# A second quarter of the input loaded by GpSimd instead of SyncE, two more quarters and one weight block asked for at other steps

## Chip, cores and metric

The kernel runs on 1 core of one Trainium2 chip. The metric is the device time of one execution in microseconds (us), the median over runs. A core has five instruction streams here: TensorE (PE, with its weight loads listed as PEld), VectorE (DVE), ScalarE (ACT), GpSimd (POOL) and SyncE (SP). SP does nothing but ask for transfers (DMAs); POOL asks for some too, on a queue of its own. Both queues are served by the same 16 DMA engines of the core.

## The reference

One layer of a mixer with adaptive layer norm: L = 2048 tokens, D = 448 channels, N = 256 states, F = 1792 hidden units, all float32.

```python
mod = (silu(c) @ w_mod).reshape(1, 6, 1, 448)        # w_mod is 448 x (6*448)
sa, ca, ga, sb, cb, gb = (mod[:, k] for k in range(6))
h = layernorm(x) * (1 + ca) + sa
x = x + ga * A_ref(h, ...)      # S4D: K[d,l] = 2 Re sum_n C exp(A dt l); long convolution by FFT; + h*D_skip
h = layernorm(x) * (1 + cb) + sb
x = x + gb * B_ref(h, ...)      # token mixing: w2.T gelu(w1.T layernorm(h) + b1) + b2
```

`A_u` is the input x (2048 x 448, 3.7 MB). `w_mod` is used in six blocks of 448 x 448, one for each of the six modulations.

## The kernel before, in words

The first half of the kernel builds the convolution kernel of the S4D layer from its 448 x 256 parameters (the "steps"), and transforms the input beside it (the "rows" and "columns"). The second half is the token MLP, a stream of large matmuls. The change lies in the first 70 us.

**Steps.** The steps are numbered s = 0 to 55 (NHALF = 56), half a group of 16 channels each. A step s consists of:

- `st_phase(s)` on PE: matmuls into two PSUM tiles, `xe` and `xg` (line 621; two buffers of each). It is issued one step ahead, so step s holds `st_phase(s + 1)`.
- `st_step(s)`: six activations on ACT (lines 677 to 682, the sines and cosines), two products on POOL (`G`, lines 684 and 685), and four on DVE (`E`, lines 686, 687, 689 and 690).
- `between()`, called between the second and the third of the DVE products: other DVE work is put in there. For 2 <= s < 8 that is `u_stats(2s)` and `u_stats(2s + 1)`, the layer norm's statistics of two of the 16 input rows in `xt` (lines 513 and 514).
- `st_kgen(s - 2)` on PE: 64 small matmuls from `E` and `G` (line 711).

Every eighth step begins with a set, `window(s)`: the exponentials of eight steps in a row (`st_exponents` on PE, `st_exp` on ACT, line 644; `st_mag2` on POOL, lines 660 and 665). The one before step 0 is called the first set here, the one before step 8 the second. In the first set, `u_stats(0)` to `u_stats(3)` are done at e = 4 to 7.

**Input.** `xt` is a tile of 128 partitions x 16 rows x 450. `x_load(r0, n, eng)` loads rows r0 to r0 + n with four DMAs, one for each group of 32 partitions, on the queue of `eng`. Four rows are called a quarter: four DMAs of 224 KB. Before the change the first quarter is asked for by POOL within `first_chain`, the second in two halves by SP after it (8 DMAs of 112 KB), the third by POOL behind step 1, the fourth by POOL behind step 2.

**Weights of the modulations.** `wm_load(k, tile)` asks for one block of `w_mod` (784 KB) on SP's queue. `modulation(k, half)` (lines 498 and 502 on PE) uses it: block 1 in steps 4 and 5, block 2 in steps 6 and 7, block 0 in the second set. `late` is a table by step: what stands at s is asked for by SP when the program comes to step s.

**Order.** The order of each engine's instructions is the order of the program (`manual_schedule`), so a wait holds up everything behind it on that engine. SP's order is written out by hand as well, up to step 8: it runs ahead of the others until a transfer has to wait for its tile, for its data or for earlier transfers. In the first set it moves the parameters of the first groups: `lex` and `lph` straight from SBUF (line 867), the rest through DRAM (`pars`, stored on line 871, read by `load` on lines 607 and 611). At s = 4 it asks for eight `lex` loads for the second set.

Of the kernel before, what the change touches and what calls it, by code (L numbers as in the profile page):

```python
# [220 lines left out]
def tile_adaln_s4d_mixer(ctx, tc, i, out):  # L221
# [20 lines left out]
    with ExitStack() as es:  # L242
        V, S, G, T = nc.vector, nc.scalar, nc.gpsimd, nc.tensor
# [53 lines left out]
        def x_load(r0, n, eng=nc.sync):  # L297
            for g in range(4):
                to = xt[32 * g : 32 * g + 32, r0 : r0 + n, 0:D]
                eng.dma_start(to, x.rearrange("(n g r) d -> g n r d", g=4, r=16)[g, :, r0 : r0 + n])  # L300
# [22 lines left out]
        def wm_load(k, tile):  # L323
            wms[k] = tile
            nc.sync.dma_start(wms[k], i["w_mod"][:, k * D : (k + 1) * D].rearrange("(q p) d -> p q d", p=PP))
# [11 lines left out]
        def wm_slot(k):  # L337
            w = wm0.rearrange("p k d -> p (k d)")[0:PP]
            return w[:, 4 * D * (k % 4) : 4 * D * (k % 4 + 1)].rearrange("p (q d) -> p q d", q=4)
# [1 line left out]


        late = {
            4: lambda: wm_load(2, wm_slot(2)),
            7: lambda: wm_load(0, wm_slot(0)),
            6: lambda: [
                nc.sync.dma_start(wu, i["WU"]),
# [114 lines left out]
        def logs(root=False):  # L462

            for a, s, u, xa, ya in tmp.values():
                S.activation(u, ya, AF.Square)
                S.activation(s, s, AF.Ln)
                S.activation(u, u, AF.Ln, bias=1.0)
            if root:
                S.activation(rs, mv[:, :, 1], AF.Ln, bias=eps_t)
                S.activation(rs, rs, AF.Exp, scale=-0.5)  # L470
            for q, (a, s, u, xa, ya) in tmp.items():
                S.activation(a, a, AF.Exp, bias=ldt[:, q : q + 1])
            tmp.clear()

        def angle():

            for a, s, u, xa, ya in tmp.values():
                S.activation(xa, ya, AF.Arctan)
# [134 lines left out]
        def load(g, exps):  # L613
            load_up(g, exps)
            load_lo(g, exps)
# [323 lines left out]
        par_load(1, par_names[2:4])  # L939
        for g in (1, 2):  # L940
            load(g, False)
        x_load(4, 2)
        x_load(6, 2)
        wm_load(1, wm_slot(1))
        remainder()

# [13 lines left out]
        def more(n):  # L960

            for _ in range(n):
                if next(rest, None) in ("logs", "end"):
                    return
# [26 lines left out]
        def window(s):  # L991
            if s:
                aside.append(True)
            angle()
            logs(s == 8)
            if s == 8:
                u_scale()
                u_table(0)
                u_table(1)

            if s == 0:
                st_exponents(s)
            for e in range(BATCH):
                st_exp(s + e)

                if e + 1 < BATCH:
                    st_exponents(s + e + 1)
                else:
                    st_phase(s)
                mellow()  # L1010
                flush(dve)
                flush(act)
                if s == 8 and e == 0:
                    tt(mod[1], mod[1], mod[2], ALU.mult)
                if s < 32:
                    more(WPACE[s // 8][e])
                if s == 0 and e >= 4:
                    u_stats(e - 4)
                if s == 8 and e in (3, 4):
                    modulation(0, e - 3)  # L1020
                if s == 8 and e == 5:

                    G.tensor_tensor(mod[0], mod[0], mod[2], ALU.mult)
                if s and e < (2 if s <= 32 else 1):
                    st_kgen(s - (2 if s <= 32 else 1) + e)
                elif e == 5:
                    if s == 8:
                        yks[0] = y0.tile([P, 32, DC], F32, tag="yk", name="yk0")
                    st_s1(s > 16)

                for k, e0 in ((4, 1), (5, 3), (3, 6)) if s == 16 else ():
                    if e in (e0, e0 + 1):
                        modulation(k, e - e0)

                if s == 8:
                    warm(7)
                if s in (8, 16):
                    some(u_rows, rows, (2, 2, 2, 2, 2, 0, 1, 1)[e])
                elif s == 24 and e != 5:
                    some(u_cols, cols, 1)  # L1040

                if s >= 40 and e == 2:
                    piece(False, True)
                if s >= 40 and e == 4:
                    piece(pieces[0] < NP, True)
                if s == 0 and e > 1:
                    st_mag2(e - 2)
                elif s and (e < 2 or s >= 32):
                    st_mag2(s + e)
                if s == 0 and e == 3:  # L1050
                    for r in range(4):
                        dsk_copy(r)
            aside.clear()
            if s == 0:

                S.activation(one, one, AF.Sin)
# [6 lines left out]
        for s in range(tail):  # L1063
            if s == 32:
                early.close()
                fp = es.enter_context(tc.tile_pool(name="fp", bufs=2))
                m2p.append(right("m2l", BATCH - 3))
                yks[1] = fp.tile([P, 32, DC], F32, name="yk1", bufs=1)
                for n in range(3):
                    pc_load(n)  # L1070
            if s % 2 == 0 and 0 < s and s // 2 + 2 < NG:
                load(s // 2 + 2, False)
            if s == 8:
                first.close()
            if s in late:
                late[s]()
            if s < NHALF and s % BATCH == 0:
                window(s)
                if s == 0:
                    gp_ = right("gp", 3)  # L1080
            if s % BATCH == 4:
                for g in range(s // 2 + 2, min(s // 2 + 6, NG)):
                    load(g, True)

            def between():
                flush(dve)
                if 2 <= s < BATCH:
                    for r in range(2 * s, 2 * s + 2):
                        u_stats(r)
                if s < len(pace):  # L1090
                    more(pace[s])

            mellow()
            if s >= NHALF:
                flush(dve)
                mellow()
            else:
                if s < 32 and s % BATCH > 1:
                    st_kgen(s - 2)
                if s % BATCH < 2:  # L1100
                    warm(10)
                if (s + 1) % BATCH:
                    st_phase(s + 1)
                elif s + 1 < NHALF:
                    st_exponents(s + 1)
                if s == 7:
                    warm(10)

                if s > 32 and s % BATCH:
                    st_kgen(s - 1)  # L1110
                st_step(s, between)
            flush(act)
            if s == NHALF:
                st_kgen(s - 1)


            if s in (1, 2):
                x_load(4 + 4 * s, 4, G)
            free = s > 7 and not st_s1(s % BATCH == BATCH - 1)
            if s + 2 < 32 and (s + 2) % BATCH > 1 and s + 2 > 5:  # L1120
                st_mag2(s + 2)

            if 3 < s < 8:
                modulation(s // 2 - 1, s % 2)
            if s == 7:
                par_load(2)

            if 8 <= s < 16 and free:
                some(u_rows, rows, 2 if s % 2 else 3)
            if s == 12:  # L1130
                par_load(3)
            if s == 16:
                spec.close()
                up = early.enter_context(tc.tile_pool(name="up", bufs=2))
                for n in range(4):
                    u_load(n)
            if 17 <= s < 32 and free:
                some(u_cols, cols, 2 if s < 24 else 3)
            if s == 31:
                flush(dve)  # L1140
                flush(act)
            if s > 32:
                piece(pieces[0] < NP and (s % 2 == 1 or s >= NHALF))
            if s == 34:

                for t in (ft, b1, b2):
                    V.memset(t, 0.0)
                nc.sync.dma_start(ft, i["FT"])
                nc.sync.dma_start(b1, i["B_b1"].rearrange("(t p) -> p t", p=P))
                nc.sync.dma_start(b2, i["B_b2"].rearrange("(t p) -> p t", p=P))  # L1150
# [52 lines left out]
    with ExitStack() as es:  # L1203
        es.enter_context(tc.manual_schedule(engines={ENG.PE, ENG.Activation, ENG.DVE, ENG.Pool}))
        V, S, G = nc.vector, nc.scalar, nc.gpsimd
# [192 lines left out]
```

## Time and profile before

| what | value |
|---|---|
| median of 3 runs | 697.69 us (696.94 to 703.69) |
| profiled execution | 699.5 us |
| its span, first to last instruction | 697.7 us |
| its mean granted TensorE clock | 0.988 |
| busy in the span | PE 646.5 us (93%), ACT 448.5 (64%), DVE 424.1 (61%), POOL 274.7 (39%) |
| DMA | 128.04 MB, mean 184 GB/s |

The profiled execution is one of its own; 1.8 us of its time lie outside the span. In the lists below every line gives the start and the duration in us, the engine, the line of the kernel, the operation and its operands; in square brackets stands how long the engine had been idle before it, and what ended that. "SPq" is a DMA instruction on SP's own queue.

### The profile page before, as it was taken

Reading aid. Unit: us, or ns where it says so; the run is one execution under the profiler, and the core shown is the slowest. Engines: PE = TensorE matmul, PEld = TensorE weight load, DVE = VectorE, ACT = ScalarE, POOL = GpSimd, SP = SyncE. Lnnn points to the kernel's source line nnn. Section 1 sums busy time; section 2 is a strip of 40 time slices with the busy share of each in tenths; the row PEclk is TensorE's granted clock in tenths of the full one; section 3 lists DMA queues with packets and bytes.
Section 4 is the critical chain, followed back from the end, with each engine's and each line's share of the span. In section 5 each row is a group of like instructions: output and inputs, shape, how many; then the busy total and the mean of one; then the engine's idle time right before and its main releaser. Section 6 shows DMA issues by size and latency. Waiting matters only on the chain.

```text
span 697.7 us, 18532 instructions
## 1 busy us (share of the span) xinstructions
PE 646.5 (93%) x7314; PEld 486.1 (70%) x7314; DVE 424.1 (61%) x811; ACT 448.5 (64%) x841; POOL 274.7 (39%) x364
## 2 busy tenths in 40 slices
PE   0868999999988899999999989999999999999997
PEld 0444454455545676676789747778999999999996
DVE  7877889787575584857744368777622354444431
ACT  5787698899879899999766568877422332222220
POOL 6694669588588767777546200000000000000000
PEclk9998999999999999999999999999999999999999
DMA  7595647588785486554579899974683445555640
GB/s 183 178 194 143 214 163 241 212 234 268 213 266 165 126 170 170 145 157 120 142 235 301 257 278 244 236 177 135 174 247 108 146 132 159 159 158 165 169 129 28
DMA packets 101894, 128.04 MB, mean 184 GB/s; under 512 B 13547, under 2 KB 85231, under 8 KB 101807
## 3 DMA queue, kind: packets, MB, share of 16 engines
q1 hardware_dynamic: 100606, 123.31, 63.0%
q0 software_dynamic: 1200, 3.54, 2.4%
q8 instruction: 58, 0.95, 0.6%
q14 instruction: 30, 0.24, 0.1%
HBM read 91.46 MB, written 34.87 MB: 181 GB/s over the span
## 4 chain that ended last, share of the span: by engine, by line
PE 68%; ACT 10%; DMA 8%; DVE 6%; issue 4%; POOL 3%; SPq 1%; DVEq 0%; ACTq 0%; POOLq 0%
PE xe L621 7%; PE acc L1222 7%; PE o L1365 6%; PE o L1364 6%; PE o L1366 6%; PE acc L1223 6%; PE acc L1224 6%; PE kg L711 6%; DMA si<-in_SK_dram 3%; PE xg L621 3%; PE pu L542 2%; PE pu L574 2%; PE vv L820 2%; PE kx L804 2%; PE vv L821 2%
## 5 line engine op out<-in xcount | busy, mean ns | idle before, releaser
L206 ACT CAST whi<-w 128x896 fp32r<-128x896 f32 x64 | 59.8, 938 | 134.9 <-PE o L1365 84.6
L215 DVE TENSOR_TENSOR wlo<-w,whi 128x896 fp32r<-128x896 f32 x64 | 68.1, 1088 | 43.1 <-ACT whi L206 36.8
L684 POOL TENSOR_TENSOR G<-mag,gs 128x512 f32<-128x512 f32 x56 | 71.9, 1283 | 50.9 <-ACT gs L680 47.1
L1222 PE MATMUL acc<-h3h,whi 128*128 128x448 f32 x224 | 82.7, 369 | 0.8 <-ACT h3h L1273 0.8
L1223 PE MATMUL acc<-h3l,whi 128*128 128x448 f32 x224 | 81.5, 364 | 0.7 <-DVE h3l L1280 0.5
L1365 PE MATMUL o<-ul,whi 128*128 128x448 f32 x224 | 81.3, 363 | 0.0
L1364 PE MATMUL o<-uh,whi 128*128 128x448 f32 x224 | 81.2, 362 | 0.0
L1224 PE MATMUL acc<-h3h,wlo 128*128 128x448 f32 x224 | 80.7, 360 | 0.0
L1366 PE MATMUL o<-uh,wlo 128*128 128x448 f32 x224 | 80.6, 360 | 0.0
L711 PEld LDWEIGHTS kg<-E,G 128*32 128x32 f32 x3584 | 56.6, 114 | 32.3 <-issue 22.2
L711 PE MATMUL kg<-E,G 128*32 128x64 f32 x3584 | 66.4, 228 | 6.7 <-issue 6.1
L685 POOL TENSOR_TENSOR G<-mag,gs 128x512 f32<-128x512 f32 x56 | 71.8, 1282 | 0.0
L621 PE MATMUL xg<-tab,lph 64*128 64x512 f32 x112 | 62.3, 556 | 5.1 <-ACT gs L680 2.4
L621 PE MATMUL xe<-tab,lph 64*128 64x512 f32 x112 | 62.2, 555 | 1.1 <-ACT gs L681 0.9
L686 DVE TENSOR_TENSOR E<-m,xe 128x512 f32<-128x512 f32 x53 | 36.4, 687 | 41.3 <-ACT xe L679 24.3
L1368 DVE SCALAR_TENSOR_TENSOR y<-o,b,mod 128x448 f32<-128x448 f32 x16 | 10.9, 684 | 80.2 <-PE o L1366 80.2
L665 POOL TENSOR_TENSOR m<-mag,w 128x512 f32<-128x512 f32 x53 | 56.0, 1056 | 4.3 <-DMA u<-us_d 0.2
L1222 PEld LDWEIGHTS acc<-h3h,whi 128*128 128x128 f32 x224 | 42.0, 188 | 13.9 <-ACT h L1278 5.6
L812 DVE TENSOR_TENSOR z<-kx,u 128x448 f32<-128x448 f32 x48 | 28.4, 620 | 27.7 <-PE kx L804 27.7
L1223 PEld LDWEIGHTS acc<-h3l,whi 128*128 128x128 f32 x224 | 42.1, 188 | 3.3 <-DVE h3l L1280 0.8
L1364 PEld LDWEIGHTS o<-uh,whi 128*128 128x128 f32 x224 | 42.0, 188 | 3.4
L621 PE MATMUL xe<-tab,lex 64*128 64x512 f32 x56 | 28.9, 531 | 16.6 <-DMA lex<-wm 15.8
(233 smaller groups left out, 1512.1 us busy)
## 6 DMA issues: line engine op xcount, KB each, us to landing
w<-in_B_w_dram SPq DMA_DIRECT2D x64, 224.0 KB
w<-in_B_w_dram SPq DMA_DIRECT2D x32, 448.0 KB
u<-us_d SPq DMA_DIRECT2D x48, 224.0 KB
yu_d<-yt SPq DMA_DIRECT2D x16, 448.0 KB
yi<-yu_d SPq DMA_DIRECT2D x32, 224.0 KB
us_d<-uo SPq DMA_DIRECT2D x16, 448.0 KB
v_d<-vt SPq DMA_DIRECT2D x32, 224.0 KB
vt<-v_d SPq DMA_DIRECT2D x16, 448.0 KB
```

Source lines behind the costliest of these rows:

```text
L206: self.nc.scalar.copy(hi, w)
L215: eng.tensor_tensor(lo, w, hi.bitcast(F32), ALU.subtract)
L621: T.matmul(out[k], lhs[r], rhs[r], start=start, stop=stop)
L684: G.tensor_tensor(Gt[:, 1], mg_, v32(sg), ALU.mult)
L685: G.tensor_tensor(Gt[:, 0], mg_, v32(cg_), ALU.mult)
L711: T.matmul(kg[32 * q : 32 * q + 32, m], Gt[:, c, d], E[:, c, d], start=h == 0 and c == 0 and m == 0, stop=h == 1 and c == 1, skip_group_ch ...
L1222: nc.tensor.matmul(acc[f], hi[:, fs], h3h[:, r], start=r == 0, stop=False)
L1223: nc.tensor.matmul(acc[f], hi[:, fs], h3l[:, r], start=False, stop=False)
L1224: nc.tensor.matmul(acc[f], lo[:, fs], h3h[:, r], start=False, stop=r == 15)
L1364: nc.tensor.matmul(o, hi[:, ks], uh[kh][:, k], start=kh == 0 and k == 0, stop=False)
L1365: nc.tensor.matmul(o, hi[:, ks], ul[kh][:, k], start=False, stop=False)
L1366: nc.tensor.matmul(o, lo[:, ks], uh[kh][:, k], start=False, stop=kh == 1 and k == 6)
```

## The change

Four edits:

1. `x_load(4, 2)` and `x_load(6, 2)` on SP, between the loads of groups 1 and 2 and `wm_load(1)`, are taken out; one `x_load(4, 4, G)` is put into the first set at e = 2 (only for s = 0), so POOL asks for the second quarter with four DMAs, ahead of its `st_mag2(0)`.
2. The third quarter is asked for behind step 0 instead of step 1.
3. The fourth quarter is asked for behind step 3 instead of step 2.
4. Block 2 of `w_mod` is asked for at s = 5 instead of s = 4, so on SP's queue it comes behind the eight `lex` loads of s = 4. `wm_load(1)` keeps its place in the program, but eight DMAs fewer stand ahead of it.

```diff
         late = {
-            4: lambda: wm_load(2, wm_slot(2)),
+            5: lambda: wm_load(2, wm_slot(2)),
             7: lambda: wm_load(0, wm_slot(0)),
...
         for g in (1, 2):
             load(g, False)
-        x_load(4, 2)
-        x_load(6, 2)
         wm_load(1, wm_slot(1))
         remainder()
...
                 if s < 32:
                     more(WPACE[s // 8][e])
+                if s == 0 and e == 2:
+                    x_load(4, 4, G)
                 if s == 0 and e >= 4:
                     u_stats(e - 4)
...
-            if s in (1, 2):
-                x_load(4 + 4 * s, 4, G)
+            if s in (0, 3):
+                x_load(12 if s else 8, 4, G)
```

## The prediction

> **What bounds the kernel now.** I read the slices and engine shares first: PE is busy 93% of the span, and the thin place is the first tenth. Then the busy time by stretch, then DVE's, PE's, POOL's and SP's lists for 8 to 70 us, and the landing times of the input's transfers. The change acts on the steps before the second set, so that stretch is the one to price. This is it, in windows of 3.4 us:
>
> ```profile
> 39.18:42.59 3.41, 1.70 (x56) 1.12 (x44) 3.34 (x9) 3.19 (x7) 3.40 (x5) 1.00 1.06 236
> 42.59:46.00 3.41, 3.41 (x71) 2.35 (x69) 3.34 (x8) 2.17 (x6) 3.40 (x6) 0.54 1.05 205
> 46.00:49.40 3.40, 2.93 (x73) 1.68 (x72) 0.90 (x2) 3.37 (x7) 3.40 (x3) 0.96 1.11 200
> 49.40:52.80 3.40, 0.00 (x0) 0.00 (x0) 1.25 (x3) 1.59 (x4) 3.32 (x5) 1.00 1.02 199
> 52.80:56.20 3.40, 3.00 (x14) 1.43 (x13) 3.33 (x9) 0.47 (x2) 1.66 (x3) 0.55 0.58 121
> 56.20:59.60 3.40, 3.40 (x59) 1.95 (x62) 3.37 (x8) 3.40 (x7) 1.33 (x2) 0.50 0.17 58
> ```
>
> The columns are length, busy PE, PEld, DVE, ACT and POOL, granted clock, DMA share and GB/s. PE stands for a whole window, the DMA engines are full from 39 to 53 us, and twice the clock is granted at about half. DVE's list says why:
>
> ```profile
> 37.92 0.69 DVE L686 TENSOR_TENSOR E<-m,xe 128x512 f32<-128x512 f32 x1 [0.41 <-ACT xe L679]
> ...
> 45.62 0.68 DVE L686 TENSOR_TENSOR E<-wm,xe 128x512 f32<-128x512 f32 x1
> 46.22 0.68 DVE L687 SCALAR_TENSOR_TENSOR E<-mag,xe 128x512 f32<-128x512 f32 x1
> 51.52 0.63 DVE L513 BATCH_NORM_STATS2 st<-xt 128x6 f32<-128x448 f32 x1 [4.62 <-DMA xt<-in_A_u_dram]
> ...
> 62.94 0.69 DVE L686 TENSOR_TENSOR E<-m,xe 128x512 f32<-128x512 f32 x1 [0.99 <-issue]
> ...
> 66.19 0.68 DVE L690 TENSOR_TENSOR E<-m,xg 128x512 f32<-128x512 f32 x1
> ```
>
> L686 opens a step; steps 2, 4 and 7 are shown. From step 2 on DVE has no gap but two: 4.62 us in step 4, where the statistics of input row 8 wait for the third quarter, and 0.99 in step 7. A step takes 3.85 us (37.92 to 45.62 is two), and DVE sets the pace. The step 7 gap is PE's lateness at half clock, through ACT:
>
> ```profile
> 61.27 0.60 ACT L677 ACTIVATE ab<-xe 128x512 f32<-128x512 f32 x1 [1.62 <-PE xe L621]
> 67.66 0.29 ACT L469 ACTIVATE rs<-mv,eps_t 128x16 f32<-128x16 f32 x1
> ```
>
> **The change part by part.** POOL and SP now:
>
> ```profile
> 15.27 0.78 POOL L857 TENSOR_TENSOR wm<-p,wm 128x256 fp32r<-128x256 f32 x1
> 17.27 0.27 POOL L660 TENSOR_TENSOR w<-mag 128x16 f32<-128x16 f32 x1 [1.23 <-ACT mag L644]
> 21.23 0.30 POOL L660 TENSOR_TENSOR w<-mag 128x16 f32<-128x16 f32 x1 [2.42 <-ACT mag L644]
> ...
> 32.32 1.32 POOL L685 TENSOR_TENSOR G<-mag,gs 128x512 f32<-128x512 f32 x1
> 35.13 1.29 POOL L684 TENSOR_TENSOR G<-mag,gs 128x512 f32<-128x512 f32 x1 [1.48 <-ACT gs L680]
> ...
> 37.60 2.20 POOL L300 DMA_DIRECT2D xt<-in_A_u_dram  x4
> ...
> 42.26 2.20 POOL L300 DMA_DIRECT2D xt<-in_A_u_dram  x4
> 44.47 1.29 POOL L684 TENSOR_TENSOR G<-mag,gs 128x512 f32<-128x512 f32 x1
> ```
>
> ```profile
> 9.37 4.53 SPq L867 DMA_DIRECT2D lex<-wm  x7
> ...
> 17.22 3.22 SPq L867 DMA_DIRECT2D lex<-wm  x5
> ...
> 30.03 6.09 SPq L300 DMA_DIRECT2D xt<-in_A_u_dram  x8
> 36.16 0.43 SPq L325 DMA_DIRECT2D wm<-in_w_mod_dram  x1
> ...
> 39.55 0.46 SPq L325 DMA_DIRECT2D wm<-in_w_mod_dram  x1
> ...
> 43.71 7.01 SPq L607 DMA_DIRECT2D lex<-pars  x1
> ```
>
> PE's list, and two pieces of the chain of work that ended last:
>
> ```profile
> 15.80 0.76 PE L621 MATMUL xe<-tab,lex 64*128 64x512 f32 x1 [15.80 <-DMA lex<-wm]
> 19.24 0.79 PE L621 MATMUL xg<-tab,lex 64*128 64x512 f32 x1 [2.68 <-DMA lex<-wm]
> ...
> 38.72 1.10 PE L711 MATMUL kg<-E,G 128*32 128x64 f32 x64
> ...
> 47.10 0.96 PE L502 MATMUL pm<-wm,scb 112*32 112x448 f32 x8
> 47.88 1.06 PE L711 MATMUL kg<-E,G 128*32 128x64 f32 x58
> 53.16 0.43 PE L711 MATMUL kg<-E,G 128*32 128x64 f32 x6 [4.23 <-issue]
> ```
>
> ```profile
> 17.22 1.98 DMA lex<-wm
> ...
> 37.66 2.15 POOL xt L300 x4
> ```
>
> *Issue time.* Four issues cost POOL 2.20 us wherever they stand. At e = 2 POOL is free from 16.05 (15.27 + 0.78): the issues end at 18.25, the product of 17.27 slips by 1 us and takes 1.5, and the next waits for ACT until 21.23. Cover 2.42 us, cost nothing. Behind step 0 POOL is free from 33.64; the issues end at 35.84, and step 1's G slips 0.7 us, which `st_kgen(1)` at 38.7 on PE does not see (G done 38.3). Behind step 3 they push step 4's G by some 1 us; its reader comes in step 6. The chain has 2.15 us of POOL's issues at 37.66 on it; I count no gain for it, since DVE has no gap there. SP sheds 6.09 us, and `wm_load(1)` moves from 36.16 to about 30.
>
> *When each quarter lands.* The landing times after issue, for the first, third and fourth quarter:
>
> ```profile
> DMA to landing us min/median/max: 5.7/6.4/7.3
> DMA to landing us min/median/max: 8.5/10.3/12.1
> DMA to landing us min/median/max: 10.5/11.6/12.4
> ```
>
> A quarter takes 1.7 us from first to fourth issue, so the first was in at most 9.0 us behind its first issue (7.3 + 1.7); the third took 13.9 (37.60 to 51.52). These are the bounds. *Third quarter:* from 33.64 it lands between 42.6 and 47.5; row 8 is asked for at 46.9 (46.22 + 0.68). The stall of 4.62 goes; 0 to 0.6 of it stays, and I take 0, because block 1 is then asked for at 30, not inside it, and block 2 later. *Second quarter:* asked for at 16, needed at 39: no wait. *Fourth quarter:* its first issue comes behind step 3's G, which ends at 47.0 now and, without the 2.20 at 42.26, near 44.7. It lands between 53.7 and 58.6. Its reader is step 6: L686 at 37.92 + 4 x 3.85 = 53.3, statistics 1.2 later, 54.5. A stall of 0 to 4.1 us. The first quarter, which ran beside other loads of about 1 MB (seven `lex`, two tables, two parameters), is the nearest row: block 2 and eight `lex` loads, 1.2 MB, run beside this one. I take 0.8.
>
> *The first set.* The second quarter's 0.9 MB now runs from about 18 to 23 us, among the `lex` and `lph` loads that feed the first exponentials.
>
> Beside the first quarter the first `lex` load needed 6.4 us (9.37 to 15.80); alone, 1.98. The difference, 4.4, is the upper bound of the slip, 0 the lower. The load PE waits for at 19.24 is issued 1.2 us behind the first input issue and is nearly through; the later ones come every 0.65 us (3.22 over 5) while a pair of exponential steps needs one only every 2 us. I take 0.8, and it shifts all that follows.
>
> The Trainium skill ("DMA: Bandwidth & Descriptors", section "Issuing engines are not separate DMA queues") speaks against the first edit: DMAs of all issuing engines share the same 16 engines, so another queue saves issue time alone. By it the move yields SP's 6.09 us and no bandwidth; the sum already counts no gain from bandwidth, and the slip above is its price.
>
> *Block 2.* It was asked for at 39.55 and is wanted on PE in step 6, then near 55. Behind the eight `lex` loads it goes out near 44. Block 1 was asked for at 36.16 and used at 47.1, so 10.9 is enough: 54.9, cost 0. If SP stands 7.01 again as at 43.71, it costs up to the whole gain. I take 0, since SP has eight transfers fewer in flight.
>
> *Sum.* -4.62 (step 4) -0.99 (step 7) +0.8 (first set) +0.8 (step 6) = -4.0 at the second set. Everything behind that is in program order and moves with it. 699.5 - 4.0 = 695.5 for an execution like the profiled one, which stands 1.8 above the median of the runs shown; against that median, 693.7.
>
> **The rivals.** *B, the whole slack comes back.* With DVE never waiting, PE does not fall to half clock, ACT's step 7 starts not at 61.27 but when step 5's products release its PSUM tiles, 37.92 + 4 x 3.85 = 53.3, plus some 1.3 for its matmuls (an estimate: a few of the 0.79 shown, overlapped): 54.6. That is 6.7 earlier, and L469 at 67.66 follows ACT, not DVE. For it: step 7's gap is PE's. Against: both new waits have to be nil. -6.7: 691.0. The clock decides: 42.59 to 46.00 got 0.54 after a window in which PE was busy 1.70 of 3.41. The Trainium skill ("TensorE: Matmul & The Clock Gate", section "What's actually happening") lets the clock fall after an idle window; here a half-idle one was enough, so the fall may return in steps 3 to 4, where PE still idles.
>
> *C, PE's halt is its own.*
>
> At 48.9 PE stops for 4.23 us inside a group of 64, whose operands were complete by 47.0 (step 3's G: 44.47 and two times 1.25), with no releaser. If that halt comes of the full DMA engines and not of the input, it returns: phase 6 at 53.2 instead of 49.5, and of DVE's 5.6 us some 3 are lost again. -5.6 + 3 + 0.8 = -1.8: 695.9. Against: DVE was stalled over the same time.
>
> *D, slower: the fourth quarter falls behind the weights.* SP, no longer held, runs ahead and asks for block 2, block 0 (784 KB each) and 512 KB of parameters by 50 us. If the engines serve these first, at the 200 GB/s of 46 to 53 us they put 4 + 2.6 us behind block 2's share, which the 13.9 holds already: landing at 44.7 + 13.9 + 6.6 = 65.2, a stall of 10.7 in step 6, -5.6 + 0.8 + 10.7 = +5.9: 703.6. It is slower from a landing past 59.3 on, 14.6 us behind the first issue. For it: the third quarter took 13.9 with one block beside it. Against: landings so far never exceeded that.
>
> **How the numbers follow.** Forecast 0.42, B 0.23, C 0.19, D 0.16. One per cent is 7 us, about what a measurement of this kernel can tell from no change. Faster by over 1% (below 690.7): six tenths of B, and a sixth of the forecast, where later stretches add a little: 0.21. Slower by over 1% (above 704.7): half of D and a little of C: 0.10. Within: 0.69. The range reaches from B with its spread, 689.5, to the nearer half of D, 701.5; the forecast alone, with the bounds of the two waits that I took at 0.8, spans 691 to 697.
>
> **What would show it.** Right: no input wait on DVE in step 4; L686 every 3.85 us from step 2 on; the second set's L469 some 4 us earlier; a wait of at most 2 us for `xt` in step 6; PE's `xg` of 19.24 within 1 us of it. Wrong: a `lex` or `lph` wait of over 2 us on PE before 29 us; a wait for `xt` in step 6 of over 4; PE's 4 us halt at another place; the second set earlier but the end not.

## The result, and the profile after

The changed kernel takes 707.77 us (median of 4 runs, 703.57 to 713.33) against 698.82 for the kernel before in the same comparison (4 runs, 696.94 to 703.69): ratio 1.0129, 95% interval 1.0092 to 1.0166. It is slower, by 1.3%; 693.7 was predicted, with a range to 701.5. The profiled execution took 707.53 us with a span of 705.8 (before 697.7) and a mean granted clock of 0.980.

PE's list over the first 76 us shows the two losses in its brackets:

```profile
15.17 0.76 PE L621 MATMUL xe<-tab,lex 64*128 64x512 f32 x1 [15.17 <-DMA lex<-wm]
20.49 0.79 PE L621 MATMUL xg<-tab,lex 64*128 64x512 f32 x1 [4.56 <-DMA lex<-wm]
...
23.16 0.76 PE L621 MATMUL xg<-tab,lex 64*128 64x512 f32 x1 [1.45 <-DMA lex<-wm]
...
62.03 1.72 PE L502 MATMUL pm<-wm,scb 112*32 112x448 f32 x8 [5.47 <-DMA wm<-in_w_mod_dram]
63.52 1.93 PE L711 MATMUL kg<-E,G 128*32 128x64 f32 x64
...
73.88 1.77 PE L542 MATMUL pu<-xt,wur 32*64 32x449 f32 x8 [3.07 <-POOL wur L529]
```

Two waits for `lex` stand in the first set where before had one of 2.68. In step 6 PE now waits 5.47 us for block 2, and what comes behind it runs at half clock: the group of 64 takes 1.93 us, against 1.10 in before's list. DVE, by contrast, does what was forecast up to step 5:

```profile
32.53 0.69 DVE L686 TENSOR_TENSOR E<-m,xe 128x512 f32<-128x512 f32 x1 [6.10 <-ACT xe L679]
...
39.86 0.69 DVE L686 TENSOR_TENSOR E<-m,xe 128x512 f32<-128x512 f32 x1 [0.41 <-ACT xe L679]
...
47.56 0.68 DVE L686 TENSOR_TENSOR E<-wm,xe 128x512 f32<-128x512 f32 x1
48.76 0.62 DVE L513 BATCH_NORM_STATS2 st<-xt 128x6 f32<-128x448 f32 x1
...
55.25 0.68 DVE L686 TENSOR_TENSOR E<-m,xe 128x512 f32<-128x512 f32 x1
59.36 0.63 DVE L513 BATCH_NORM_STATS2 st<-xt 128x6 f32<-128x448 f32 x1 [2.83 <-DMA xt<-in_A_u_dram]
```

Steps 2 to 6 open every 3.85 us (39.86 to 55.25 is four of them), the statistics in step 4 wait for nothing, and the next wait is the one in step 6. Why block 2 is late, from SP's and POOL's lists and the chain of work that ended last:

```profile
41.49 0.42 SPq L607 DMA_DIRECT2D lex<-pars  x1
...
44.99 0.48 SPq L611 DMA_DIRECT2D lex<-pars  x1
45.52 0.43 SPq L325 DMA_DIRECT2D wm<-in_w_mod_dram  x1
...
52.64 0.97 SPq L325 DMA_DIRECT2D wm<-in_w_mod_dram  x1
```

```profile
15.45 2.18 POOL L300 DMA_DIRECT2D xt<-in_A_u_dram  x4
17.64 0.25 POOL L660 TENSOR_TENSOR w<-mag 128x16 f32<-128x16 f32 x1
...
45.93 2.20 POOL L300 DMA_DIRECT2D xt<-in_A_u_dram  x4
```

```profile
45.52 16.46 DMA wm<-in_w_mod_dram
...
62.03 1.72 PE pm L502 x8
63.75 1.71 PE kg L711 x64
...
67.76 0.37 ACT ks L725
...
70.79 0.20 ACT rs L469
...
73.88 1.77 PE pu L542 x8
```

Block 2 is asked for at 45.52 and is 16.46 us on its way; the fourth quarter follows it 0.4 us later on POOL's queue. The chain then leads from block 2 through the modulation and the group of 64 to ACT's copy of that group (L725), and through it to L469 and the second set. The windows show the DMA engines full until about 60 us, then PE falling to half clock (columns as in the prediction):

```profile
52.80:56.20 3.40, 3.16 (x74) 1.87 (x74) 3.33 (x8) 3.36 (x7) 3.32 (x5) 1.00 1.06 211
56.20:59.60 3.40, 0.36 (x3) 0.00 (x0) 0.57 (x2) 3.09 (x6) 3.25 (x4) 1.00 1.06 193
59.60:63.00 3.40, 0.97 (x8) 0.40 (x12) 3.33 (x8) 0.00 (x0) 1.49 (x2) 0.56 0.40 100
63.00:66.40 3.40, 3.40 (x73) 2.21 (x65) 2.87 (x7) 0.53 (x1) 0.00 (x0) 0.50 0.41 127
```

Five places give the account of the 8.1 us of span. The first of them in after is 32.53, shown above, and the others follow here; the rows of before for the first, the fourth and the last come next, and those for the second and third stand in the prediction (61.27 and 67.66):

```profile
56.43 0.60 ACT L677 ACTIVATE ab<-xe 128x512 f32<-128x512 f32 x1 [0.27 <-PE xe L621]
70.69 0.29 ACT L469 ACTIVATE rs<-mv,eps_t 128x16 f32<-128x16 f32 x1
92.79 0.60 ACT L644 ACTIVATE mag<-xe 128x512 f32<-128x512 f32 x1 [0.27 <-issue]
L1222 PEld LDWEIGHTS acc<-h3h,whi x4: 186/187/188, 416.5 to 418.6; 128*128 128x128 f32 x4
```

```profile
30.60 0.69 DVE L686 TENSOR_TENSOR E<-m,xe 128x512 f32<-128x512 f32 x1 [2.73 <-ACT xe L679]
86.76 0.60 ACT L644 ACTIVATE mag<-xe 128x512 f32<-128x512 f32 x1 [0.27 <-issue]
L1222 PEld LDWEIGHTS acc<-h3h,whi x14: 186/187/188, 408.5 to 419.7; 128*128 128x128 f32 x14
```

| place | before | after | difference | change since the last place |
|---|---|---|---|---|
| step 0, first product on DVE | 30.60 | 32.53 | +1.9 | +1.9 |
| step 7 on ACT | 61.27 | 56.43 | -4.8 | -6.8 |
| second set, L469 | 67.66 | 70.69 | +3.0 | +7.9 |
| second set, L644 | 86.76 | 92.79 | +6.0 | +3.0 |
| token MLP, first weights | 408.5 | 416.5 | +8.0 | +2.0 |

The gain was made, 6.8 us of it, and lost again between step 6 and the second set.

### The profile page after: what moved, and what is told of

The parts are those of the page before. It is cut to its first block, busy times and chain, and to the rows that moved or that the text cites. A ratio compares the mean times of both kernels' runs of the same rounds, so it can differ in the third digit from the quotient of the medians.

```text
span 705.8 us, 18532 instructions
## 1 busy us (share of the span) xinstructions
PE 647.8 (92%) x7314; PEld 486.6 (69%) x7314; DVE 422.4 (60%) x811; ACT 448.5 (64%) x841; POOL 276.2 (39%) x368
## 4 chain that ended last, share of the span: by engine, by line
PE 69%; ACT 9%; DMA 8%; DVE 4%; issue 4%; POOL 3%; SPq 2%; DVEq 0%; ACTq 0%; POOLq 0%
PE acc L1222 6%; PE o L1364 6%; PE o L1366 6%; PE xe L621 6%; PE o L1365 6%; PE acc L1224 6%; PE acc L1223 6%; PE kg L711 5%; PE pu L542 3%; PE vv L820 2%; DMA wm<-in_w_mod_dram 2%; PE pu L574 2%; PE vv L821 2%; PE kx L804 2%; PE xg L621 2%
## 5 line engine op out<-in xcount | busy, mean ns | idle before, releaser
L1366 PEld LDWEIGHTS o<-uh,wlo 128*128 128x128 f32 x224 | 42.1, 188 | 3.2
L1224 PEld LDWEIGHTS acc<-h3h,wlo 128*128 128x128 f32 x224 | 42.0, 188 | 3.3
```

Source lines behind the costliest of these rows:

```text
L1224: nc.tensor.matmul(acc[f], lo[:, fs], h3h[:, r], start=False, stop=r == 15)
L1366: nc.tensor.matmul(o, lo[:, ks], uh[kh][:, k], start=False, stop=kh == 1 and k == 6)
```

## The experiments

The theory was that the loss comes from block 2 (edit 4) and from the first set (edit 1). The rivals were that another edit is to blame, that the clock is, or that the DMA engines are full whatever the order. Each kernel's own runs of the kernel before (medians 698.54 to 699.39) are its reference. The ratio is not simply the quotient of two medians: for the first row that would be 1.0067.

| kernel | median us | ratio, 95% interval |
|---|---|---|
| edits 1, 2, 3 (edit 4 undone) | 703.22 | 1.0047 (1.0022 to 1.0072) |
| edit 4 alone | 710.93 | 1.0170 (1.0151 to 1.0189) |
| edits 2, 3, 4 (edit 1 undone) | 713.16 | 1.0204 (1.0182 to 1.0226) |
| all four, PE filled in step 6 | 706.59 | 1.0112 (1.0091 to 1.0133) |
| edit 1 alone | 702.61 | 1.0056 (1.0027 to 1.0086) |
| edits 1, 2, 3, second quarter at e = 7 | 703.78 | 1.0068 (1.0041 to 1.0096) |
| edits 2, 3 | 700.06 | 1.0009 (0.9981 to 1.0036) |
| all four, fourth quarter behind step 2 | 708.90 | 1.0121 (1.0072 to 1.0169) |
| all four, fourth quarter behind step 5 | 709.43 | 1.0146 (1.0119 to 1.0173) |
| all four, block 2 behind block 1, second quarter at e = 7 | 703.39 | 1.0062 (1.0038 to 1.0085) |
| block 2 behind block 1 alone | 699.98 | 1.0031 (1.0004 to 1.0059) |
| edits 2, 3, block 2 behind block 1 | 704.68 | 1.0074 (1.0046 to 1.0102) |

### Edit 4 undone, and edit 4 alone

```diff
-            5: lambda: wm_load(2, wm_slot(2)),      # the kernel after
+            4: lambda: wm_load(2, wm_slot(2)),      # edit 4 undone
```

> The changed kernel with its fourth edit undone: block 2 is asked for at s = 4 again, ahead of the eight lex loads; the other three edits stay. Theory 1 (the late block 2 is what made the change slower: PE stood 5.47 us for it in step 6, fell to half clock twice, and threw away what the earlier input had won): no wait of PE for w_mod in step 6, L469 of the second set at or below 66 us instead of 70.69, the whole 8 to 14 us below the changed kernel, so 693 to 699, at or under the kernel before. Theory 2 (the slip of the first set, 2.5 us, and the fourth quarter's stall in step 6, 2.83 us, are what counts; PE's wait only hides them): at most 4 us below the changed kernel, 702 or more.

Measured: 703.22 us, 4.5 less than the kernel after. Block 2 is used without a wait, and step 6's wait for `xt` is 1.11 us. PE's list:

```profile
58.91 0.96 PE L502 MATMUL pm<-wm,scb 112*32 112x448 f32 x8
```

So about half of the loss hung on edit 4. Theory 1 had the wait right and hoped for more; by its total the kernel lies nearer to theory 2. What stays is in the first set: here PE's wait for `lex` was 7.60 us.

> The kernel before with the fourth edit alone: block 2 at s = 5, the input asked for as before. Theory 1: PE waits for w_mod in step 6 by 4 us or more and runs at half clock after it; slower than before by 3 to 10 us, although block 2 no longer stands in front of the third quarter's last transfer and the stall of 4.62 us in step 4 shrinks to below 2. Theory 2: within 2 us of before, as DVE's stall covers the wait.

Measured: 710.93 us, 12.4 above its reference, more than either theory gave: alone, edit 4 costs more than all four together. The stall in step 4 shrinks to 2.82 us, and not below 2. SP's list of this kernel shows why:

```profile
43.68 6.53 SPq L607 DMA_DIRECT2D lex<-pars  x1
...
55.52 0.34 SPq L325 DMA_DIRECT2D wm<-in_w_mod_dram  x1
```

With the second quarter's 8 DMAs still on it, SP stands 6.53 us at one `lex` load and waits some 4 us more for earlier loads to land, and block 2 is asked for at 55.52, 16 us later than before. PE then waits 5.12 us for it.

### Edit 1 undone

```diff
+        x_load(4, 2)
+        x_load(6, 2)
         wm_load(1, wm_slot(1))
...
-                if s == 0 and e == 2:
-                    x_load(4, 4, G)
```

> The changed kernel with its first edit undone: the second quarter on SP's queue, ahead of wm_load(1), as before; edits 2 to 4 stay. If the second quarter at 16 us is what delays the first set, PE's xg waits of 20.49 and 23.16 go back to one at about 19 and 20.7, DVE's first L686 stands near 30.5 instead of 32.53. Theory 1: the late block 2 stays, so the end gains at most 2 us on the changed kernel and stays above the one before. Theory 2: 3 us or more are gained.

Measured: 713.16 us, 5.4 above the kernel after, where both theories had it no slower. The first set is back at a wait of 2.6 us, but block 2 goes out at 57.51, and the waits list has:

```profile
PE pm L502 <- DMA wm<-in_w_mod_dram: 10.5, 1, 10.5
```

The edits therefore do not add. Edit 1 costs 3.5 to 4 us alone and saves 5.4 in company, because it takes from SP's queue what holds edit 4's block 2. My figure that SP would no longer stand was right for the change as a whole.

### The fourth quarter elsewhere

The kernel after asks for block 2 in time (45.52), so something else holds it. Two kernels move the fourth quarter, which follows it at 45.93.

```diff
-            if s in (0, 3):      # the kernel after
+            if s in (0, 2):      # first kernel
+            if s in (0, 5):      # second kernel
```

> The changed kernel with its third edit undone: the fourth quarter behind step 2, so about 3 us ahead of block 2's request, which stays at s = 5. If block 2 is late because the fourth quarter overtakes its last packets, it has to come behind all of that quarter and PE's wait on L502 stays at 3 us or more, while DVE's wait of 2.83 us in step 6 goes; the whole within 3 us of the changed kernel. If the collision alone made it late, the wait goes below 1 us and 4 us or more are won.

Measured: 708.90 us, no different from the kernel after. Step 6's wait for `xt` is gone, and block 2, now behind the quarter (asked for at 50.68), is waited for still: 5.01 us. So edit 3 by itself is not the cause. More this run does not tell: block 2 also went out 5.2 us later than in the kernel after, and was 13.1 us on its way (50.68 to 63.81).

> The kernel after with one step moved: the fourth quarter is asked for behind step 5 instead of step 3, some 7.7 us later, so it is no longer on its way when block 2 (asked for near 45.5 us) is. Theory T (block 2's last packets were held behind the fourth quarter's): block 2 lands within some 9 us, PE's 5.47 us wait for it falls below 1, and the price appears on DVE instead, a wait for xt in step 6 of 6 to 11 us. Rival (block 2 is late because of its place behind the lex loads on SP's queue, whatever POOL asks for): PE's wait for block 2 stays at 4 to 6 us and DVE's wait comes on top. Total in both 708 to 714 us, so the waits decide, not the total.

Measured: 709.43 us; the waits have changed places. PE's, SP's, POOL's and DVE's rows of it:

```profile
58.11 0.96 PE L502 MATMUL pm<-wm,scb 112*32 112x448 f32 x8
```

```profile
47.19 0.47 SPq L325 DMA_DIRECT2D wm<-in_w_mod_dram  x1
```

```profile
54.97 2.20 POOL L300 DMA_DIRECT2D xt<-in_A_u_dram  x4
```

```profile
67.66 0.63 DVE L513 BATCH_NORM_STATS2 st<-xt 128x6 f32<-128x448 f32 x1 [9.51 <-DMA xt<-in_A_u_dram]
```

Block 2 is asked for 1.7 us later than in the kernel after, and PE uses it without a wait 10.9 us behind its request (58.11 - 47.19). In the kernel after it took 16.46. The one edit between the two kernels is the place of the quarter's 0.9 MB, which in this kernel comes 7.8 us behind block 2 instead of 0.4. So block 2 was held by the fourth quarter, and not by its place behind the `lex` loads. Two of the kernels above say the same, and in them PE waits for block 2, so that its end is known: with edit 4 alone and with edit 1 undone block 2 went out some 13.6 us behind the fourth quarter, and took 9.4 us (55.52 to 64.90) and 9.5 (57.51 to 67.02), although block 0 was asked for 4.4 us behind it. The prediction's 10.9 thus holds where no quarter of the input starts beside block 2.

The Trainium skill ("DMA: Bandwidth & Descriptors", section "Queues, rings and completion order") says that each DMA engine takes turns between the queues it has work for, a packet at a time. If nothing else counted, block 2 (0.8 MB) and the quarter (0.9 MB) would then both be in after some 8 us at the 211 GB/s of 52.80 to 56.20, near 54 (an estimate). That both queues are served at once agrees with the trace of the kernel after: from 46 to 52 us SP's queue moved 0.89 MB and POOL's 0.39, from 52 to 58 it was 0.65 and 0.53. That block 2 is in by 54 does not: 62.03. From 46 to 62 SP's queue moved 2.2 MB, far more than block 2 and the eight `lex` loads ahead of it (0.8 and 0.4 MB). So part of what was asked for behind block 2, block 0 (52.64) among it, was moved before the last of block 2. Why that came so late is not shown.

### PE filled while it waits

```diff
+            if s == 6:
+                warm(45)
```

`warm(45)` is 45 matmuls on ones, ahead of block 2's modulation, whose result is not used.

> The changed kernel with 45 more of the filling matmuls (those of line 633, results unused) on PE ahead of step 6's modulation, so that PE is busy through most of its wait for block 2: 45 of 0.127 us are 5.7 us. It prices the half clock apart from the wait. If the clock is a cost of its own, the granted clock stays full from 59 to 66 us, L711 behind the modulation takes 1.1 and not 1.93 us, and 2 to 5 us of the changed kernel's time come back. If the wait alone counts, its time stays within 1 us.

Measured: 706.59 us. The windows of this kernel show that the clock stays up through step 6:

```profile
56.00:60.00 4.00, 3.75 (x37) 2.66 (x29) 1.94 (x4) 3.72 (x9) 3.77 (x5) 1.00 1.07 204
60.00:64.00 4.00, 3.66 (x36) 2.73 (x37) 3.59 (x8) 0.94 (x2) 2.50 (x2) 1.00 0.65 146
64.00:68.00 4.00, 4.00 (x88) 2.56 (x84) 2.86 (x7) 1.67 (x5) 0.00 (x0) 1.00 0.33 111
```

The half clock of step 6 is gone. In the two profiled executions the stretch from block 2's modulation on PE to L469 on ACT is 6.5 us (63.33 to 69.78) against 8.7 in the kernel after (62.03 to 70.69), so the half clock there was worth some 2.2 us. Of the whole time 1.2 us are gained, which the intervals (1.0091 to 1.0133 here, 1.0092 to 1.0166 for the kernel after) do not tell from nothing. Half clock also comes back in the second set (0.50 from 73.20 to 76.60), so this run does not price all of it. Block 2 is as late as before, 16.2 us on its way (47.13 to 63.33): in step 6 the wait is the larger part of the loss, and the clock follows it.

### Edit 1 alone, and the second quarter five places later

> The kernel before with the first edit alone: the second quarter by POOL at e = 2 of the first set, nothing else moved. If that transfer delays the lex loads as in the changed kernel, PE waits 4 us or more for lex before its first xg (2.68 before) and DVE's first L686 comes 2 to 5 us later; the third quarter, asked for at 37.6 with block 2 close behind, still stalls DVE in step 4. Theory 1 in its new form (two losses: the first set's slip by edit 1, PE's wait for block 2 by edit 4): 1 to 5 us slower than before. Rival (edit 1 helps, as the run without it was 5 us slower than the changed kernel): 1 to 5 us faster than before.

Measured: 702.61 us, 3.5 above its reference. PE's list has the slip, at the place that the kernel after has it:

```profile
22.18 0.79 PE L621 MATMUL xg<-tab,lex 64*128 64x512 f32 x1 [6.37 <-DMA lex<-wm]
```

22.18 stands against 19.24 before: 2.9 us. Over the six kernels with the second quarter at e = 2 this wait was 4.56 and 1.45 (after), 6.37 (here), 7.60 (edit 4 undone), 6.24 (PE filled), 7.27 (fourth quarter behind step 2) and 6.50 (behind step 5). The first product of step 0 came 1.9 to 4.3 us later than in before, least of all in the kernel after.

One thing came out otherwise than expected: with edit 1 alone DVE waits for `xt` nowhere, in step 4 neither. PE halts all the same, 3.63 us inside a group of 64, and DVE opens step 6 3.15 us late behind ACT:

```profile
55.26 0.43 PE L711 MATMUL kg<-E,G 128*32 128x64 f32 x6 [3.63 <-issue]
```

```diff
-                if s == 0 and e == 2:
+                if s == 0 and e == 7:
                     x_load(4, 4, G)      # with edits 2 and 3; block 2 at s = 4
```

> The changed kernel with block 2 at s = 4 again, and the second quarter asked for by POOL at e = 7 of the first set instead of e = 2, so behind the lex and lph loads. If the slip of the first set is the rest of the loss, PE's first xg stands near 19 us again, DVE's first L686 near 31, and the whole at 692 to 697, below the kernel before. If the slip does not matter, 701 to 705 as with block 2 at s = 4 alone.

Measured: 703.78 us: missed. The slip is gone, as PE's row shows, but the end is no earlier, since other transfers are late instead, by DVE's rows:

```profile
19.11 0.79 PE L621 MATMUL xg<-tab,lex 64*128 64x512 f32 x1 [2.92 <-DMA lex<-wm]
```

```profile
39.58 0.63 DVE L513 BATCH_NORM_STATS2 st<-xt 128x6 f32<-128x448 f32 x1 [0.85 <-DMA xt<-in_A_u_dram]
...
49.44 0.63 DVE L513 BATCH_NORM_STATS2 st<-xt 128x6 f32<-128x448 f32 x1 [2.07 <-DMA xt<-in_A_u_dram]
```

### Edits 2 and 3, and block 2 earlier

> The kernel before with the second and third edit alone: third quarter behind step 0, fourth behind step 3; the second quarter on SP and block 2 at s = 4 as before. No slip of the first set. If SP's eight issues and the order of the weights behind them are harmless, the stall of step 4 goes and 693 to 697 come out; if they make block 1 or block 2 late (PE waits on L502), 699 or more.

Measured: 700.06 us, the same as its reference. The input's stall of 4.62 us in step 4 is gone (0.61 is left in step 3, for the second quarter), and nothing of the end comes of it: PE now waits for block 2, and halts for 1.86 and 1.01 us in its groups of 64.

```profile
59.07 0.96 PE L502 MATMUL pm<-wm,scb 112*32 112x448 f32 x8 [1.98 <-DMA wm<-in_w_mod_dram]
```

So three kernels ask for block 2 earlier, straight behind block 1:

```diff
-            4: lambda: wm_load(2, wm_slot(2)),
...
         wm_load(1, wm_slot(1))
+        wm_load(2, wm_slot(2))
```

> The kernel after with two steps moved: block 2 is asked for straight behind block 1, ahead of the rest of the parameters, and the second quarter at e = 7 of the first set instead of e = 2. Theory (the price of the change is block 2's place and the first set's slip; both moves take it away): no wait of PE for block 2, PE's xg wait of the first set back at 2.7 to 3, 694 to 698 us. Rival (the transfers of 28 to 55 us fill the engines whatever their order, and the wait appears at another tile, as the run with the second quarter at e = 7 showed): a wait of 2 us or more for xt in step 4 or 6 and 699 to 704 us.

> The kernel before with block 2 asked for straight behind block 1 (some 3 us earlier than at s = 4) and nothing else changed. Theory (who is first on the queues is served first, the others wait): no wait of PE for block 2; the third quarter, whose stall in step 4 is 4.62 us before, lands later by up to 1.5 us: 698 to 701 us. Rival (order does not matter while there is slack behind block 2): same as before, within 0.5 us.

> The kernel before with the second and third edits (third quarter behind step 0, fourth behind step 3) and block 2 asked for straight behind block 1. With the two edits alone 700.1 us, PE waited 1.98 us for block 2 and halted 1.9 and 1.0 us in its groups of 64. Theory (what kept those two edits from paying was block 2's late landing): PE's wait gone, 694 to 698 us. Rival (the engines are full and another transfer is late instead, the fourth quarter in step 6 or the third in step 4): a wait of 1 to 4 us on DVE for xt, 698 to 702 us.

Measured: 703.39, 699.98 and 704.68 us. No one waits for block 2 in them, and none is faster than before. The theory missed in the first and the last. In the second it had the total right and the stall wrong: the total is 0.6 us above its reference, at the edge of its interval (1.0004 to 1.0059), and the stall in step 4 is 3.5 us and not longer than 4.62. The last kernel shows where the time went; SP's, PE's and DVE's rows (its line numbers are one less):

```profile
41.49 9.34 SPq L606 DMA_DIRECT2D lex<-pars  x1
```

```profile
55.39 0.47 PE L620 MATMUL xe<-tab,lph 64*128 64x512 f32 x1 [0.71 <-DMA lph<-pars]
57.93 0.76 PE L620 MATMUL xg<-tab,lph 64*128 64x512 f32 x1 [2.07 <-DMA lph<-pars]
```

```profile
61.34 0.69 DVE L685 TENSOR_TENSOR E<-m,xe 128x512 f32<-128x512 f32 x1 [5.93 <-issue]
```

Now the parameters `lph` (32 and 64 KB), asked for behind the two blocks, are late for PE, which has also halted 2.89 us ahead of them, and DVE waits 5.93 us behind PE and ACT. `xt` costs 0.2 us. The rival came true in the first kernel (2.45 us of wait for `xt` in step 4); in the last it had the tile and the total wrong. What the three have in common is that some transfer is late in every order, and only the tile changes. No order among the kernels run beats the kernel before.

## Why the prediction was wrong

By its own steps:

- **Issue time: right.** The four issues at e = 2 took 2.18 us, the product behind them started at 17.64 instead of 17.27. Block 1 was asked for at 29.66 ("about 30").
- **Third quarter, -4.62: right.** No wait in step 4, steps at 3.85 us. Up to step 7 even more came back: 61.27 to 56.43 with 1.9 us of slip inside it is 6.8, which is rival B's 6.7. The half clock that B feared for steps 3 to 4 did not return: the granted clock was 1.00 in every window from 35.78 to 59.60.
- **First set, +0.8: mis-sized.** It measured +1.9 at the first product of step 0 (30.60 to 32.53). PE's first matmul was 0.6 us earlier here (15.17 against 15.80), so the slip itself is some 2.5; over the six kernels the product came 1.9 to 4.3 later. The bound, 4.4, was worked out rightly, and passed a little by the wait of 7.60 (4.9 above 2.68); the choice near its lower end was the mistake. I argued from when the loads are issued and not from what they meet on the engines: the `lex` load asked for at 17.52 was 5.50 us on its way (chain of the kernel after), against 1.98 in before.
- **Fourth quarter, +0.8: mis-sized** at 2.83 (59.36), inside its bounds of 0 to 4.1. It came 13.4 us behind its first issue, near the upper bound of 13.9. (That bound was a little low: this quarter's own landing time in before, 12.4, and the 1.7 of its issues make 14.1.)
- **Block 2, 0: this step failed.** Its request was forecast near 44 and came at 45.52, and SP did not stand. But "10.9 is enough" was taken from block 1, which PE did not wait for, while the fourth quarter had just been put on the engines beside block 2. It took 16.46 where 9.4 to 10.9 were measured without that company, and its use, wanted at 56.6, came at 62.03: 5.47 us of wait, then half clock, and 7.9 us lost between step 7 and L469. The prediction did see that the quarter and block 2 run beside each other, and priced it for the quarter only. The run with the fourth quarter behind step 5 shows that pairing as the cause of block 2's lateness. For the time, undoing edit 4 gave back 4.5 of the 8.9 us; no run took away the pairing without making something else late.
- **Rival D** had the place, the pairing and the sign right and the tile wrong: not the quarter fell far behind the weights, but the weights behind the quarter. Its 703.6 was for 10.7 us of stall on DVE; the loss was PE's.
- **Rival C** (PE's halt is its own) is not seen in the kernel after, where PE has no such halt ahead of step 6. But with edit 1 alone it is there, 3.63 us, with no wait for `xt` at all, and in the last kernel of the experiments, with 0.2 us of such a wait, it is 1.86 and 2.89. So the halt needs no stall on the input, as this rival said. What makes it stays open.

Of the 8.1 us the table above puts 3.0 (1.9 less 6.8 and 7.9 more) on steps named here. The last 5 us, in the second set and behind it, were not isolated by a run. PE's list has 3.07 us of wait for `wur` at 73.88, with `wur` late because L469 was late, and the windows have half clock again:

```profile
73.20:76.60 3.40, 2.72 (x22) 0.89 (x26) 2.46 (x6) 2.28 (x6) 3.02 (x7) 0.57 0.06 20
76.60:80.00 3.40, 3.40 (x75) 2.51 (x69) 1.26 (x3) 1.02 (x3) 2.95 (x5) 0.50 0.70 255
```

In before both of these windows had the full clock (1.00). That the delay feeds the idle time and the idle time the clock is argued from these rows, not shown.

## What to carry to other kernels

Where the DMA engines are full, moving one transfer earlier makes another one late: price each change of order on every tile that is in flight beside it, and on the engine that waits for that tile, not only on the tile that is moved. A transfer's duration taken from one place of a trace holds only for the company it had there; a large transfer that starts beside yours costs it several microseconds even when yours was asked for first. And edits to one queue do not add: what edit 4 cost depended on what edit 1 had taken off that queue.

## What the runs showed that was not expected

- A block of 784 KB asked for 0.4 us ahead of another queue's 0.9 MB took 16.46 us; with that transfer 7.8 us behind it, at most 10.9, and with it 13.6 us ahead, 9.4 and 9.5.
- Loads of `lex` beside a quarter on POOL's queue made PE wait 4.6 to 7.6 us, against 1.6 to 3.3 without it.
- SP stood 9.34 and 10.19 us at a single `lex` load behind two blocks of weights, and 6.53 with the second quarter on its queue. With the quarter off its queue it still stood 6.72 with block 2 ahead of the `lex` loads (edit 1 alone); with block 2 behind them all eight took 4 us (41.49 to 45.52, the kernel after).
- A stall of 4.62 us on the engine that sets the pace of the steps, removed by edits 2 and 3, moved the end by nothing that can be measured (ratio 0.9981 to 1.0036).
